# The last head pair's products with v of the first batch, moved ahead of late weight norms and of the second batch's scores in TensorE's order

## The chip, the cores and the metric

One core of a Trainium2 chip runs the whole program. Its engines each work through an instruction stream of their own, in order: TensorE (PE in the profile; its weight loads are listed as PEld), VectorE (DVE), ScalarE (ACT), GpSimd (POOL) and SyncE (SP, which here only starts DMA transfers). The metric is the device time of one execution in microseconds, taken as the median of several.

## The reference

Eight batches of sliding-window attention with position bias, whose output, laid out as 4608 tokens by 512 features, goes through a bilinear feed-forward layer:

```python
scores = scale * np.matmul(q, k.transpose(0, 1, 3, 2))          # 8 batches, 8 heads, 576 x 576, head size 64
scores = np.where(mask, scores + bias[None], -1000000000.0)     # window of 128 keys
attn = np.exp(scores - max); attn = attn / (sum + 1e-09)
x = np.matmul(attn, v)            # then (B*S, H*D) = (4608, 512)
out = (x @ w_a * (x @ w_b)) @ w_out    # 512 -> 1536 -> 512
```

All inputs are float32 numbers. The three weight matrices reach the kernel as the 64-bit integers that hold them.

## The kernel before

**Precision.** Each operand of the feed-forward layer is scaled by a power of two and split into a high and a low float16 part; three products (high·high, high·low, low·high) are added in PSUM. The scales come from norms: for each block of weights, squares are summed over the rows by a TensorE product with a matrix of ones (`up_norms`, line 152), VectorE takes the maximum (`up_scales`, line 158), GpSimd turns it into a power of two, and only then can the block be split.

**Preparing the weights.** There are 12 blocks f of the two up matrices and 6 pairs of blocks of the down matrix. For each block SP loads the raw words (line 119), ScalarE and VectorE take the words apart (lines 130, 131, 133), GpSimd adds two pieces (line 135, two instructions a block), ScalarE squares (line 141), TensorE sums the squares (line 156, four matmuls a block, called "norms" here), and after two blocks the four splits follow (ScalarE line 149, VectorE line 150). The norms of a pair of blocks, one even and one odd, share one PSUM tile `wn_ps`. The raw words lie in three buffers, so the load of block f+3 waits for the norms of block f. The whole is a Python generator, `weights`, of which other code draws steps.

**The first batch.** `first_attention` (line 526) runs batch 0 in float32 as 16 stages: 4 head pairs, 4 banks of query tiles each. A stage has the score products (line 569), bias and minimum on VectorE (line 580), exponentials on ScalarE (line 581), transposes of the probabilities on TensorE (line 587), and a copy of them out of PSUM (line 595). Behind the fourth bank of a pair come `pv`: reciprocals of the sums (lines 603, 604), a product that spreads them over PSUM (`rin_ps`, line 610), their copy to SBUF (ScalarE, line 614), the products with v (line 501, 14 float32 matmuls a pair; the trace has two records for each float32 matmul), and the scaled result x (VectorE, line 619), its squares (line 420 or 425) and, once all four pairs are there, the sum of squares over features (`n_ps`, line 515), the scale g of the hidden layer, and the split of x into `xs` (lines 435 and 436). The pairs' probabilities lie by turns in the buffers `phl` (pairs 0 and 2) and `pT` (1 and 3), so a product `x_ps<-pT,v` in the second half is that of the last pair. In each stage `other(0.5)` is called twice, which draws 0.75 steps of `weights` each.

**What sits in the same stretch.** Behind batch 0's attention come its up layer (`first_up`, line 836, products named `up_ps`), and woven into it the attention of batch 1 (`attention`, scores at lines 374 to 383) and the rest of `weights`.

**What sets the order.** The order in which the Python code emits is only a wish in this part: for TensorE, VectorE, ScalarE and GpSimd a scheduler places each instruction by its own estimate of when operands and buffers are ready, and by a priority (`tc.high_priority`). Only SP's order is kept as written here. From batch 1's feed-forward layer on TensorE's order is kept as written too. `tc.issue_after(i)` forbids the scheduler to place an instruction ahead of instruction i on its engine. PSUM has eight banks: two tagged `ch`, three `ef`, and three `at`. The `at` banks serve in turn the score tiles, the norms `wn_ps` and the two `n_ps` tiles of batch 0, which are opened when the first two pairs' squares are there and stay open until the last pair's are added.

Of the kernel before, what the change touches and what calls it, by code (L numbers as in the profile page):

```python
# [23 lines left out]
P = 128  # L24
NPAIR = H // 2
NKC = DM // P
# [16 lines left out]
PRIO = 2000  # L43
# [3 lines left out]
def attention_then_bilinear_ffn(ctx: ExitStack, tc: tile.TileContext, qT, kT, vP, w_a, w_b, w_out, rel, slopes2, outT):  # L47
# [104 lines left out]
    def up_norms(f, sq, ps):  # L152

        norms = ps[:, 2 * P * (f % 2):2 * P * (f % 2) + 2 * P].rearrange("p (m f) -> p m f", f=P)
        for c in range(NKC):
            pe.matmul(norms, ones16, sq[:, :, c * P:(c + 1) * P], start=(c == 0), stop=(c == NKC - 1))

    def up_scales(g, ps):

# [100 lines left out]

    class State:
        pass

    def load_v(b):

# [98 lines left out]
    def scores(o, bi):  # L364

        ps = ps_at.tile([P, 512], F32, tag="at", name="sc_ps")
        t = work.tile([P, 512], F32, tag="t", name="t", bufs=4)
        for i, c in BANKS[bi]:
            w = TILES[i][1]
            qq, kk = slice(64 * i, 64 * i + 64), slice(64 * i + 64 - w, 64 * i + 64)  # L370
            if o.b == 1:
                for e in range(2):
                    r = slice(64 * e, 64 * e + 64)
                    pe.matmul(ps[r, c:c + w], o.q[r, qq], o.k[r, kk], start=True, stop=True)
                continue
            for ks, last in ((o.kh, False), (o.kl, True)):
                for e in range(2):
                    pe.matmul(ps[64 * e:64 * e + 64, c:c + w], o.qs[:, e, qq], ks[:, e, kk], start=not last, stop=last)  # L378
        for i, c in BANKS[bi]:
            pc, w = TILES[i]  # L380
            n = o.n
            vec.tensor_tensor_reduce(out=t[:, c:c + w], in0=ps[:, c:c + w], in1=o.bias[:, WIN - w:WIN], scale=-0.125 if o.b == 1 else o.neg, scalar=3.0e38, op0=ALU.add, op1=ALU.min, accum_out=o.mn[:, n:n + 1])  # L382
            act.activation(t[:, c:c + w], t[:, c:c + w], AF.Exp, bias=o.mn[:, n:n + 1], scale=-1.0, accum_out=o.sm[:, n:n + 1])  # L383
            o.parts.append((n, t[:, c:c + w], pc, w))
            o.n += 1
# [104 lines left out]
    def each_pv(xp, vts, pts):  # L490

        for b in range(5):
            for rows, oc, blocks in by_keys(b):
                w = 64 * len(blocks)
                bank0, o0 = oc < 512, oc % 512
                first = oc == 0 if bank0 else b == 3
                last = b == 3 if bank0 else b == 4
                for n, (vt, pt) in enumerate(zip(vts, pts)):
                    for h in range(2):
                        c = 512 + 64 * h if b == 4 else 64 * (4 * h + b)  # L500
                        pe.matmul(xp[oc // 512][64 * h:64 * h + 64, o0:o0 + w], vt[0:rows, c:c + 64], probs(pt, rows, blocks, h), start=(n == 0 and first), stop=(n == len(vts) - 1 and last), skip_group_check=True)  # L501

    def pv(p, st, o, vhl):
        xp = new_x_ps()
# [19 lines left out]
    def first_attention(weights, rate):  # L524
# [74 lines left out]
        def pv(p, pt):  # L599


            rin = small.tile([P, QT], F32, tag="rin", name="rin0")
            vec.tensor_scalar(out=rin, in0=sums[p], scalar1=1e-9, scalar2=None, op0=ALU.add)
            vec.reciprocal(rin, rin)
            yield
            rp = [ps_ch.tile([P, 512], F32, tag="ch", name="rin_ps") for _ in range(2)]
            for i in range(QT):
                for e in range(2):
                    r = slice(64 * e, 64 * e + 64)
                    pe.matmul(rp[i // 8][r, 64 * (i % 8):64 * (i % 8) + 64], rin[r, i:i + 1].to_broadcast([64, 64]), ident[r, r], start=True, stop=True)  # L610
            r = first.tile([P, S], F32, tag="rin0", name="rin0", bufs=1)
            x = st.v[:, p, 0:S]
            for n, (c, w) in enumerate(halves_of_x):
                act.copy(r[:, c:c + w], rp[n][:, 0:w])
            xp = [ps_ch.tile([P, 512], F32, tag="ch", name="x_ps") for _ in range(2)]
            each_pv(xp, (st.v[:, p, :],), (pt,))
            yield
            for n, (c, w) in enumerate(halves_of_x):
                vec.scalar_tensor_tensor(out=x[:, c:c + w], in0=xp[n][:, 0:w], scalar=st.sv, in1=r[:, c:c + w], op0=ALU.mult, op1=ALU.mult)
            yield  # L620
            square_x(p, st, x, first if p == 2 else work if p == 3 else None)
            yield

        bias(0)
        n = 4 * NPAIR
        t = exponentials(0, 0, products(0, 0))
        beside = iter(())
        for k in range(n):
            p, bi = k // 4, k % 4
            ps = products((k + 1) // 4, (k + 1) % 4) if k + 1 < n else None  # L630
            other(0.5)
            if bi == 1 and p + 1 < NPAIR:
                bias(p + 1)
            tp = transposed(t)
# [7 lines left out]
                v_scale(st)  # L642
            if bi == 3:
                beside = pv(p, pts[p % 2])
            other(0.5)

        with tc.high_priority(offset=PRIO):
            next(beside)
        other(0.5)
        with tc.high_priority(offset=PRIO):  # L650
            for _ in beside:
                pass
            hidden_scale(st)
            for _ in split_x(st, True, False):
                pass
        states[0] = st

    def attention():
# [402 lines left out]
```

## Time and profile before

| | before |
|---|---|
| median of 3 runs | 1005.48 us (1005.28 to 1111.78) |
| the profiled execution: its own time | 1006.61 us |
| its span, first to last instruction | 1004.8 us |
| TensorE busy | 965.3 us, 96% |
| VectorE, ScalarE, GpSimd busy | 673.8, 649.2, 307.2 us |
| mean granted TensorE clock | 0.988 |

A row of the page or of a timeline gives start, duration, engine, source line, operation and tiles, and in brackets how long the engine had been idle before and what ended that. Rows of the window table give the busy time of each engine in a stretch of the span, and under PEclk the clock that TensorE was granted, 1.00 being full. Batch 0's attention takes the first 75 us or so, its feed-forward layer ends near 216 us, and the other seven batches fill the rest.

### The profile page before, as it was taken

The page shows a single profiled execution, that of the slowest core. Times are in us where ns is not written, and L with a number is a line of the kernel's source. Part 1 is how long each engine was busy: PE and PEld are TensorE (multiplying, and loading weights), DVE is VectorE, ACT ScalarE, POOL GpSimd, SP SyncE. Part 2 cuts the span into 40 slices and gives each one's busy share as a digit, 9 for nine tenths or more (in the row PEclk, how much of TensorE's full clock was granted, in tenths as well). Part 3 has the DMA queues.
Part 4 walks back from the last instruction along what each step waited for, and adds up shares of the span by engine and source line. Part 5 has one row for each costly group of instructions (what it writes and reads, how often), then busy time and mean ns, then how long its engine had stood idle before and what let it go on. Part 6 is the DMA issues. An engine that isn't in the chain of part 4 may idle for free.

```text
span 1004.8 us, 23888 instructions
## 1 busy us (share of the span) xinstructions
PE 965.3 (96%) x9339; PEld 750.9 (75%) x9339; DVE 673.8 (67%) x1833; ACT 649.2 (65%) x1715; POOL 307.2 (31%) x345
## 2 busy tenths in 40 slices
PE   7789879999999999999999999999999999999998
PEld 6567656777777777777787777777777777877776
DVE  5888999657878566775878687666677476524530
ACT  6886779657767756777767767677666766413321
POOL 3643463104565321352226112230223022211100
PEclk7799999999999999999999999999999999999999
DMA  8317733564444442472624642464326632210001
GB/s 318 119 74 266 234 112 73 124 166 81 100 90 96 141 90 43 97 172 66 126 49 107 172 90 45 95 178 107 80 62 106 161 67 43 49 37 7 2 13 36
DMA packets 148433, 102.83 MB, mean 102 GB/s; under 512 B 120032, under 2 KB 128352, under 8 KB 147296
## 3 DMA queue, kind: packets, MB, share of 16 engines
q1 hardware_dynamic: 138816, 91.77, 37.6%
q10 hardware_dynamic: 9504, 9.54, 2.9%
q8 instruction: 73, 1.20, 0.5%
q14 instruction: 40, 0.33, 0.1%
HBM read 48.33 MB, written 9.44 MB: 57 GB/s over the span
## 4 chain that ended last, share of the span: by engine, by line
PE 62%; DVE 11%; DMA 6%; ACT 6%; issue 2%; POOL 1%; SPq 0%; ACTq 0%; DVEq 0%
PE ch L836 19%; PE dn_ps L932 16%; PE p L836 14%; PE up_ps L836 8%; PE x_ps L501 3%; PE sc_ps L378 3%; DVE phl L400 2%; DMA pT<-phl 2%; DMA v<-in_vP 1%; DMA qk<-in_kT 1%; ACT phl L399 1%; DVE t L382 1%; ACT t L383 1%; DVE xs L436 1%; DMA qst<-qkl 1%
## 5 line engine op out<-in xcount | busy, mean ns | idle before, releaser
L836 PEld LDWEIGHTS <-wup 128*128 128x128 f16 x4224 | 407.9, 98 | 120.5 <-issue 14.8
L932 PE MATMUL dn_ps<-h,wdn 128*128 128x288 f16 x2016 | 254.3, 286 | 0.0
L932 PEld LDWEIGHTS <-wdn 128*128 128x128 f16 x2016 | 193.9, 98 | 51.8
L836 PE MATMUL ch<-xs,wup 128*128 128x288 f16 x1536 | 221.7, 286 | 0.9 <-ACT rc L861 0.6
L836 PE MATMUL up_ps<-xs,wup 128*128 128x288 f16 x1536 | 195.1, 286 | 6.1 <-DVE rc L785 4.6
L836 PE MATMUL p<-xs,wup 128*128 128x288 f16 x1152 | 172.6, 286 | 0.0
L891 POOL TENSOR_TENSOR rc<-rc,row 128x288 f32<-128x288 f32 x64 | 62.4, 975 | 279.7 <-DVE row L889 263.8
L400 DVE SCALAR_TENSOR_TENSOR phl<-t,rin,phl 128x192 f16<-128x192 f32 (+2 forms) x252 | 110.0, 477 | 18.9 <-ACT phl L399 18.7
L383 ACT ACTIVATE t<-t,mn 128x192 f32<-128x192 f32 (+2 forms) x252 | 107.2, 427 | 23.4 <-DVE mn L382 23.0
L829 ACT CAST h<-rc 128x576 f16<-128x576 f32 x96 | 64.2, 669 | 68.2 <-DVE rc L896 37.5
L399 ACT ACTIVATE phl<-t,rin 128x192 f16<-128x192 f32 (+2 forms) x252 | 88.7, 425 | 23.3 <-DMA pT<-phl 11.1
L830 DVE TENSOR_TENSOR h<-rc,h 128x576 f16<-128x576 f32 x90 | 71.2, 791 | 32.8 <-ACT h L829 32.0
L382 DVE CUSTOM_DVE_ANT_0 t<-sc_ps,bias,neg 128x192 f32<-128x192 f32 (+2 forms) x216 | 73.7, 389 | 8.4 <-PE sc_ps L378 8.4
L135 POOL TENSOR_TENSOR wup<-wup,wdn 128x512 int32<-128x512 int32 x36 | 54.7, 1541 | 45.6 <-ACT wdn L130 13.2
L937 ACT ACTIVATE row<-dn_ps,oi 128x288 f32<-128x288 f32 x56 | 27.7, 494 | 56.0 <-PE dn_ps L932 55.9
L873 ACT ACTIVATE row<-ch,g 128x288 f32<-128x288 f32 x64 | 31.9, 498 | 48.8 <-PE ch L836 48.8
L436 DVE TENSOR_TENSOR xs<-v,xs 128x576 f16<-128x576 f32 x52 | 48.4, 944 | 21.9 <-ACT xs L435 21.8
L360 POOL TENSOR_SCALAR bias<-rel_sb,ninv,sl_sb 128x192 f32<-128x192 f32 x24 | 21.4, 892 | 123.7 <-DVE mn L382 123.7
L868 DVE TENSOR_TENSOR rc<-p,rc 128x288 f32<-128x288 f32 x64 | 29.1, 454 | 44.1 <-PE p L836 34.8
L896 DVE SCALAR_TENSOR_TENSOR rc<-rc,g,ch 128x288 f32<-128x288 f32 x64 | 32.6, 510 | 23.6 <-PE ch L836 23.4
L383 ACT ACTIVATION_READ_ACCUMULATOR t<-t,mn 128x1 f32 x252 | 47.7, 189 | 0.0
L430 POOL TENSOR_TENSOR xq<-xq,sq 128x576 bf16<-128x576 bf16 x22 | 29.5, 1343 | 56.1 <-ACT sq L429 56.1
(151 smaller groups left out, 1311.7 us busy)
## 6 DMA issues: line engine op xcount, KB each, us to landing
v<-in_vP SPq DMA_DIRECT2D x8, 1280.0 KB, 6.0
out<-row ACTq DMA_DIRECT2D x60, 144.0 KB, 1.8
qk<-in_qT SPq DMA_DIRECT2D x28, 288.0 KB, 4.0
qk<-in_kT SPq DMA_DIRECT2D x28, 288.0 KB, 4.5
wdn<-in_w_a SPq DMA_DIRECT2D x12, 512.0 KB, 5.2
wdn<-in_w_b SPq DMA_DIRECT2D x12, 512.0 KB, 6.2
wdn<-in_w_out SPq DMA_DIRECT2D x12, 512.0 KB, 4.3
qst<-qkh SPq DMA_DIRECT2D x24, 144.0 KB, 2.8
```

The lines of the kernel that those rows point to most:

```text
L135: pool.tensor_tensor(out=t[:, m, :], in0=t[:, m, :], in1=low[:, m, :], op=ALU.add)
L382: vec.tensor_tensor_reduce(out=t[:, c:c + w], in0=ps[:, c:c + w], in1=o.bias[:, WIN - w:WIN], scale=-0.125 if o.b == 1 else o.neg, scalar= ...
L383: act.activation(t[:, c:c + w], t[:, c:c + w], AF.Exp, bias=o.mn[:, n:n + 1], scale=-1.0, accum_out=o.sm[:, n:n + 1])
L399: act.activation(phl[:, 0, pc:pc + w], e, AF.Copy, scale=s)
L400: vec.scalar_tensor_tensor(out=phl[:, 1, pc:pc + w], in0=e, scalar=s, in1=phl[:, 0, pc:pc + w], op0=ALU.mult, op1=ALU.subtract)
L436: vec.tensor_tensor(out=xs[:, n, 1, :, :], in0=src, in1=xs[:, n, 0, :, :], op=ALU.subtract)
L829: act.copy(h[:, f, :, 0, :], hid)
L830: eng.tensor_tensor(out=h[:, f, :, 1, :], in0=hid, in1=h[:, f, :, 0, :], op=ALU.subtract)
L836: pe.matmul(ps[:, 0:HT], wup[:, a[0], a[1], wi, k, :], xs[:, b, xi, k, :], start=(first and n == 0), stop=(last and n == len(ks) - 1), ski ...
L891: pool.tensor_tensor(out=x0, in0=x0, in1=mid, op=ALU.mult)
L896: vec.scalar_tensor_tensor(out=x1, in0=x1, scalar=st.g, in1=ch, op0=ALU.mult, op1=ALU.mult)
L932: pe.matmul(ps[:, 0:HT], wdn[:, f, wi, e * P:(e + 1) * P], h[:, f, t, hi, :], start=(m == 0 and n == 0), stop=(m == NF - 1 and n == 2))
```

## The change

`each_pv` returns its last matmul, and `first_attention` keeps that of the last head pair in `last_pv`. Two groups of instructions then may stand on TensorE only behind it: the norms of weight blocks whose step is drawn after that point, and all scores of batch 1. The draws themselves move too: stage 15, the last, no longer draws, and the draws around the last pair are put together into one, `other(1.0)`, behind the whole of the last pair's work with its hidden scale and split. The number of steps drawn in all stays 24.

```diff
     def up_norms(f, sq, ps):
...
-        for c in range(NKC):
-            pe.matmul(norms, ones16, sq[:, :, c * P:(c + 1) * P], start=(c == 0), stop=(c == NKC - 1))
+        with tc.issue_after(last_pv[0].ins) if last_pv[0] else ExitStack():
+            for c in range(NKC):
+                pe.matmul(norms, ones16, sq[:, :, c * P:(c + 1) * P], start=(c == 0), stop=(c == NKC - 1))
...
             if o.b == 1:
-                for e in range(2):
-                    r = slice(64 * e, 64 * e + 64)
-                    pe.matmul(ps[r, c:c + w], o.q[r, qq], o.k[r, kk], start=True, stop=True)
+                with tc.issue_after(last_pv[0].ins):
+                    for e in range(2):
+                        r = slice(64 * e, 64 * e + 64)
+                        pe.matmul(ps[r, c:c + w], o.q[r, qq], o.k[r, kk], start=True, stop=True)
...
-            each_pv(xp, (st.v[:, p, :],), (pt,))
+            last = each_pv(xp, (st.v[:, p, :],), (pt,))
+            if p == NPAIR - 1:
+                last_pv[0] = last
...
-            other(0.5)
+            if k < n - 1:
+                other(0.5)
...
-            other(0.5)
-
-        with tc.high_priority(offset=PRIO):
-            next(beside)
-        other(0.5)
+            if k < n - 1:
+                other(0.5)
+
         with tc.high_priority(offset=PRIO):
             for _ in beside:
                 pass
             hidden_scale(st)
             for _ in split_x(st, True, False):
                 pass
+        other(1.0)
```

Line numbers behind line 154 are larger by 1 to 7 in the changed kernel: norms 157, scores of batch 1 378, products with v 505, transposes 592, spread reciprocals 615, their copies 619, x 626, its squares 429 and 433.

The first place is TensorE's order after the last scores of batch 0, at the products with v of the third pair (`x_ps<-phl`). Before:

```order
L515 MATMUL n_ps<-xq,ones_73 128x512
L587 MATMUL tr_ps<-ident,t 128x128 x4
L515 LDWEIGHTS ones_73
L515 MATMUL n_ps<-xq,ones_73 128x64
L374 MATMUL sc_ps<-qkl,qkh 64x64 x2
L374 MATMUL sc_ps<-qkl,qkh 64x128 x2
L374 MATMUL sc_ps<-qkl,qkh 64x192 x2
L501 MATMUL x_ps<-phl,v 64x128 x4
L501 MATMUL x_ps<-phl,v 64x256 x4
```

The same place in the changed kernel:

```order
L520 MATMUL n_ps<-xq,ones_73 128x512
L592 MATMUL tr_ps<-ident,t 128x128 x4
L520 LDWEIGHTS ones_73
L520 MATMUL n_ps<-xq,ones_73 128x64
L505 MATMUL x_ps<-phl,v 64x128 x4
L505 MATMUL x_ps<-phl,v 64x256 x4
```

The first three score tiles of batch 1 (`sc_ps<-qkl,qkh`) have left this place; the norms of block 5, which stood just ahead of the first row before, have left it too.

The second place is TensorE's order at the last pair's products with v. Before, the norms of block 6 are the last thing ahead of them:

```order
L156 LDWEIGHTS ones_73
L156 MATMUL wn_ps<-wdn,ones_73 128x256
L501 MATMUL x_ps<-pT,v 64x128 x4
L501 MATMUL x_ps<-pT,v 64x256 x4
L501 MATMUL x_ps<-pT,v 64x128 x2
L501 MATMUL x_ps<-pT,v 64x64 x4
```

In the changed kernel products of the up layer stand ahead of them, and norms (of block 5) behind:

```order
L843 MATMUL up_ps<-xs,wup 128x288
L505 MATMUL x_ps<-pT,v 64x128 x4
L505 MATMUL x_ps<-pT,v 64x256 x4
L505 MATMUL x_ps<-pT,v 64x128 x2
L505 MATMUL x_ps<-pT,v 64x64 x4
L157 LDWEIGHTS ones_73
L157 MATMUL wn_ps<-wdn,ones_73 128x256
```

Ahead of the last pair's products stood, before, two groups of norms (blocks 5 and 6) and two of scores that now stand behind; the norms of blocks 6 and 7 and the scores follow among the next hundred matmuls of the up layer. Over the whole program both kernels issue the same instructions on every engine, and SP's order is the same.

The third place is ScalarE's order in the same stretch; `rin` with a number (745 before, 741 now) is the last pair's reciprocals, copied from PSUM. Before:

```order
L595 COPY pT<-tr_ps 128x512
L130 ACTIVATE wdn<-wdn 128x1024
L149 ACTIVATE wup<-wup,sup 128x2x256 x4
L383 ACTIVATE t,sm<-t,mn 128x64
L383 ACTIVATE t,sm<-t,mn 128x128
L383 ACTIVATE t,sm<-t,mn 128x192
L141 ACTIVATE wdn<-wup 128x2x512
L425 ACTIVATE sq<-v 128x576
L614 COPY rin_745<-rin_ps 128x512
L614 COPY rin_745<-rin_ps 128x64
L141 ACTIVATE wdn<-wup 128x2x512
```

In the changed kernel:

```order
L130 ACTIVATE wdn<-wdn 128x1024
L600 COPY pT<-tr_ps 128x512
L141 ACTIVATE wdn<-wup 128x2x512
L429 ACTIVATE sq<-v 128x576
L141 ACTIVATE wdn<-wup 128x2x512
L619 COPY rin_741<-rin_ps 128x512
L619 COPY rin_741<-rin_ps 128x64
```

The splits of line 149 and the exponentials of batch 1 have moved behind. The copy of transposed probabilities now stands behind a conversion of weights (line 130), and the two copies of the last pair's reciprocals stand behind the second squares of weights (line 141) instead of ahead of them.

More of the change, by code (lines that the diff above doesn't have):

```diff
@@ L262, in attention_then_bilinear_ffn @@
         pass
+    last_pv = [None]
     def load_v(b):
@@ L496, in each_pv @@
                 first = oc == 0 if bank0 else b == 3
-                last = b == 3 if bank0 else b == 4
+                ends = b == 3 if bank0 else b == 4
                 for n, (vt, pt) in enumerate(zip(vts, pts)):
@@ L500, in each_pv @@
                         c = 512 + 64 * h if b == 4 else 64 * (4 * h + b)
-                        pe.matmul(xp[oc // 512][64 * h:64 * h + 64, o0:o0 + w], vt[0:rows, c:c + 64], probs(pt, rows, blocks, h), start=(n == 0 and first), stop=(n == len(vts) - 1 and last), skip_group_check=True)
+                        last = pe.matmul(xp[oc // 512][64 * h:64 * h + 64, o0:o0 + w], vt[0:rows, c:c + 64], probs(pt, rows, blocks, h), start=(n == 0 and first), stop=(n == len(vts) - 1 and ends), skip_group_check=True)
+        return last
     def pv(p, st, o, vhl):
```

## The prediction

> **What bounds the kernel now.** I read the page first, then the windows, then TensorE's waits, then the timelines around the moved instructions.
>
> ```profile
> span 1004.8 us, 23888 instructions
> PE   7789879999999999999999999999999999999998
> 53.90:72.10 18.20, 13.82 (x157) 10.30 (x156) 14.79 (x34) 13.49 (x34) 9.31 (x12) 0.91 0.07 25
> 72.10:97.00 24.90, 24.90 (x212) 18.93 (x210) 22.11 (x46) 18.48 (x41) 7.15 (x8) 1.00 0.59 228
> 97.00:122.00 25.00, 21.74 (x178) 16.12 (x177) 23.97 (x44) 18.02 (x41) 10.56 (x10) 1.00 0.77 238
> 122.00:170.00 48.00, 39.47 (x392) 29.10 (x391) 45.81 (x101) 40.33 (x91) 25.69 (x19) 1.00 0.36 100
> 170.00:216.00 46.00, 44.06 (x451) 33.50 (x449) 28.54 (x98) 29.45 (x90) 8.52 (x7) 1.00 0.65 136
> ```
>
> After the stretch's length come busy TensorE, weight loads, VectorE, ScalarE and GpSimd, the granted clock and the transfers. TensorE is the bound nearly everywhere; a change that moves its instructions and adds none is worth what it takes from or adds to its idle time and its slow-clock time. There are two stages with such time near the change. From 53.9 to 72.1 TensorE is busy 13.82 of 18.2 us, at a mean clock of 0.91. From 97 to 170 it is idle 3.3 + 8.5 = 11.8 us, and there VectorE is busy 23.97 of 25 and 45.81 of 48: that stage belongs to VectorE, which prepares weights, evicts products and does batch 1's softmax. TensorE's waits in the two:
>
> ```profile
> PE up_ps L836 <- DVE rc L785: 4.6, 2, 2.3
> PE wn_ps L156 <- DVE mn L382: 3.1, 1, 3.1
> PE wn_ps L156 <- ACT wdn L141: 2.6, 3, 1.5
> PE wtot L101 <- ACT t L383: 1.8, 1, 1.8
> PE x_ps L501 <- DVE vhl L296: 1.5, 1, 1.5
> ```
>
> The second row is the one that the change touches: norms wait 3.1 us for the minima of batch 1's scores (line 382), which hold the one `at` bank that is left. Behind that wait stand the last pair's products:
>
> ```profile
> 53.87 0.61 PE L156 MATMUL wn_ps<-wdn,ones 128*128 128x256 bf16 x4
> 54.32 0.38 PE L515 MATMUL n_ps<-xq,ones 128*128 128x512 bf16 x1
> 56.07 0.88 PE L374 MATMUL sc_ps<-qkl,qkh 64*64 64x64 f32 x12 [0.40 <-DVE wtop L161]
> 56.87 1.97 PE L501 MATMUL x_ps<-phl,v 128*64 128x128 f32 x28
> 60.83 0.87 PE L374 MATMUL sc_ps<-qkl,qkh 64*64 64x192 f32 x8
> 61.53 1.25 PE L610 MATMUL rin_ps<-ident,rin 64*64 64x64 f32 x36
> 67.57 0.61 PE L156 MATMUL wn_ps<-wdn,ones 128*128 128x256 bf16 x4 [3.14 <-DVE mn L382]
> 68.11 3.34 PE L501 MATMUL x_ps<-pT,v 128*64 128x128 f32 x28
> 71.39 0.85 PE L156 MATMUL wn_ps<-wdn,ones 128*128 128x256 bf16 x4
> 72.08 1.63 PE L836 MATMUL up_ps<-xs,wup 128*128 128x288 f16 x12
> 66.00:68.00 2.00, 0.43 (x4) 0.31 (x4) 1.51 (x6) 1.57 (x4) 0.00 (x0) 1.00 0.00 0
> 70.00:72.00 2.00, 2.00 (x20) 1.55 (x17) 0.72 (x2) 0.46 (x2) 0.00 (x0) 0.52 0.00 0
> ```
>
> The same 28 records take 1.97 us for the third pair and 3.34 for the last: right after the 3.14 us of idle time the granted clock falls to 0.52. So the wait costs 3.14, and the slow clock 1.37 on these products, in all 4.5 us in front of the last x.
>
> **The change part by part.** *Removed.* The last pair's products no longer stand behind norms 5 and 6 and two groups of scores. Their own inputs are then late next: the copied reciprocals (ScalarE) and the transposed probabilities (VectorE, line 595). The rows that feed them:
>
> ```profile
> 55.33 0.68 DVE L161 TENSOR_REDUCE wtop<-wn_ps 128x4 f32<-128x512 f32 x1
> 55.93 1.21 DVE L133 SCALAR_TENSOR_TENSOR wup<-wdn,wup 128x1024 int32<-128x1024 int32 x1
> 57.06 1.40 DVE L150 SCALAR_TENSOR_TENSOR wup<-wup,sup 128x512 f16<-128x512 f32 x2
> 59.72 0.68 DVE L131 TENSOR_SCALAR wup<-wdn 128x1024 int32<-128x1024 int32 x1
> 63.16 3.80 DVE L150 SCALAR_TENSOR_TENSOR wup<-wup,sup 128x512 f16<-128x512 f32 x3
> 71.28 0.94 DVE L619 SCALAR_TENSOR_TENSOR v<-x_ps,sv,rin 128x512 f32<-128x512 f32 x2 [2.60 <-PE x_ps L501]
> 62.77 2.98 POOL L135 TENSOR_TENSOR wup<-wup,wdn 128x512 int32<-128x512 int32 x2 [0.17 <-issue]
> 56.17 0.57 ACT L595 COPY pT<-tr_ps 128x512 f32<-128x512 f32 x1
> 56.63 1.20 ACT L130 ACTIVATE wdn<-wdn 128x1024 int32<-128x1024 uint32 x1
> 63.70 0.67 ACT L614 COPY rin<-rin_ps 128x512 f32<-128x512 f32 x2
> 65.78 1.06 ACT L141 ACTIVATE wdn<-wup 128x1024 bf16<-128x1024 f32 x1 [1.42 <-POOL wup L135]
> ```
>
> *Added.* On ScalarE the copies (0.67) stood ahead of the second line-141 squares; now they stand behind them, and those wait for GpSimd's second pair of adds, which waits for VectorE's second line 133. So the chain is: VectorE starts its first line 133 at 55.4 (the maximum of line 161 at 55.33 no longer stands ahead of it) and ends it at 56.6; two splits 1.40, line 131 0.68, a small sum 0.2 and the second line 133 1.21 bring it to 60.1. GpSimd's first pair of adds runs beside this; the row at 63.16 has three splits beside such a pair in 3.80, 1.27 each, against 0.7 each at 57.06, so three instructions beside adds cost up to 1.6 more: 60.1 to 61.7. Adds 2.98: 63.1 to 64.7. Squares 1.06: 64.2 to 65.8. Copies 0.67: 64.8 to 66.4. TensorE could start the last pair there; it waited for its norms until 68.11 before. I take 66.2, toward the upper end, since the row at 63.16 has the same two engines on the same kinds of instructions. At 1.97 us the products end at 68.2, against 71.45 (68.11 + 3.34): the last x comes 3.2 us earlier (2.9 to 4.7 by the ends).
>
> For the new gaps: at the third pair TensorE now waits for the copy of line 595, behind line 130 on ScalarE: 56.17 + 1.20 + 0.57 = 57.9, where it started at 56.87; the scores that filled this place are gone, so 2.2 us are idle from 55.7. The third pair then ends at 59.9, transposes and 12 up products take the 2.0 that lie between 58.84 and 60.83 before, and the spread reciprocals wait for VectorE until 61.3 to 62.9 (second line 133, then x of the third pair): up to 1.0 idle; with their 1.25 and six up products (0.8) the last pair's place is reached at 64 to 65: up to 1.4 idle. None is as long as 3.14, the one length that the trace shows with a fall of the clock; its bound is therefore 0 to 1.37 us for one group of products, and I take 0, with the upper end in the range. [...]
>
> *Moved, TensorE.* From 53.87 TensorE has, in the changed order, the last pair done at 68.2, then norms 5, and goes on with the 12 products of the up layer when x is scaled: 68.2 + 0.94 = 69.1. At this place it stood at 72.08 before. But it owes what has moved behind: scores 0.80 (56.07 to 56.87) and 0.70 (60.83 to 61.53), norms 6 0.54 (67.57 to 68.11) and norms 7 at full clock 0.45 (53.87 to 54.32), 2.5 in all. 69.1 + 2.5 = 71.6 against 72.08: a gain of 0.5, by the ends of the chain from 1.9 gained to 1.1 lost (66.4 + 1.97 + 1.37 + 0.94 + 2.5 = 73.2).
>
> *Moved, VectorE.* It too has done less at its line 619:
>
> ```profile
> L150 DVE SCALAR_TENSOR_TENSOR wup<-wup,sup x20: 734/744/1780, 52.9 to 132.0; 128x512 f16<-128x512 f32 x20
> L382 DVE CUSTOM_DVE_ANT_0 t<-sc_ps,bias 128x192 f32<-128x192 f32 x22 | 7.2, 347 | 0.0
> 76.23 0.33 SPq L268 DMA_DIRECT2D v<-in_vP  x1
> 147.85 2.27 POOL L830 TENSOR_TENSOR h<-rc,h 128x576 f16<-128x576 f32 x1
> ```
>
> It owes one maximum 0.68, three splits at 0.74, five minima at 0.35 at most: 4.7 us. It gets 3.2 of it back by starting line 619 earlier, and is 1.5 us behind. From 72.1 to 97 it had 24.9 - 22.11 = 2.8 us of idle time, which can take this debt, as far as the work is there to be done; what is left meets the stage from 97 to 170 where it is full. Bounds: 0 to 1.5 us lost; I take 0.5.
>
> *Queues passed.* SP's order is the same, but its transfer of v for batch 1 at 76.23 waits for the last split of x (line 436), and the raw words of blocks 8 to 10 are queued behind it. With x 3.2 us earlier it starts near 73. That gives nothing by itself where VectorE is full; it is a rival below. Behind it the load of block 10 waits for norms 7, now about 83 on TensorE instead of 72; the transfers before it still run until then. GpSimd's order moves one line 830 (2.27) from between its last adds of weights, at 147.85, to a later place: 0 to 2.3 us gained ahead of the scale of the down weights (`wtot`, 1.8 us of TensorE waiting). I count nothing, because VectorE feeds those adds.
>
> *Sum.* -0.5 + 0.5 = 0 us. From 216 us on nothing is changed, so the rest passes through as it is. The profiled execution has 1006.61 us (1004.8 of span), the median of the runs is 1005.48; taking the change from either gives the same time, and I forecast against the median: **1005.5 us**. A difference of less than 2%, about 20 us, is what a measurement of this kernel would call no change.
>
> **The rivals.** *Forecast, no change (chance 0.50):* 1004 to 1007. The 4.5 us in front of the last x go, but some 4 us of new, shorter waits come, on ScalarE and VectorE.
>
> *Faster, the early x feeds the weights (0.25).* The transfer of v and of the raw words starts 3.2 us earlier, the weights of blocks 8 to 10 are ready earlier, and TensorE's 11.8 us of waits from 97 to 170 shrink by that: 1005.5 - 3.2 = 1002, at best 1005.5 - 4.5 = 1001. For it speaks that norms wait 2.6 us for squares of weights; against it that VectorE, which takes the words apart, has no free time there (45.81 of 48).
>
> *Slower, ScalarE's order gives the gain back and VectorE's debt arrives whole (0.22).* Place: the copies behind line 141. If the last pair's products start no earlier than 68.11, the point from which it decides, TensorE owes 2.5 us with only the 1.37 of the slow clock saved, and VectorE's 4.7 us come into its full stage with at most 2.8 taken by idle time: 1005.5 + 1.2 to 1005.5 + 4.7, the middle about 1008.5. For it speaks the chain above, whose upper end lies only 1.7 us below 68.11. [...]
>
> *The change does not reach the chip as written (0.03):* the order shows that it does; what is left here are effects far from the place, at either sign.
>
> **How the numbers follow.** The likeliest case gives 1005.5. The range takes the faster case to 1001.5 and the slower to 1009.0; it leaves out about 0.1. Nothing in these cases comes near 20 us, so within 2% has 0.97, faster 0.01, slower 0.02, the last for disturbed runs such as the 1111.78.
>
> **What the profile will show.** If I am right, the wait of `wn_ps` for line 382 near 64 us is gone; the last pair's products start at 65 to 67 and take about 2.0 us; just ahead of them ScalarE's line 141 waits for GpSimd; the third pair's products start near 57.9 after an idle 2 us; and TensorE's waits from 97 to 170 sum to 11 to 13 us. A last pair at 68 or later, or a clock of 0.5 there, means the slower case; waits of under 9 us from 97 to 170 mean the faster one. The forecast is wrong if the span moves by more than 4 us, or if idle time changes behind 216 us.

## The result, and the profile after

The changed kernel is slower: 1013.92 us (median of 6 runs, 1011.36 to 1015.38) against 1004.96 us for the kernel before beside it. The ratio is 1.0089 (95% interval 1.0074 to 1.0104), about 9 us. That is within 2%, as predicted, but above the predicted range (1001.5 to 1009.0), and no case with a sizeable chance held it. One execution of the kernel before (1111.78 us) and one of the first experiment (1643.23 us) ran in a slow state of the chip and are left out of the ratios. The profiled execution of the changed kernel has 1014.11 us of its own; the first line of its page and its windows, in the columns of the prediction:

```profile
span 1012.3 us, 23889 instructions
53.90:72.10 18.20, 13.74 (x139) 10.28 (x139) 12.02 (x20) 8.92 (x17) 7.67 (x10) 0.81 0.06 24
72.10:97.00 24.90, 24.81 (x211) 18.47 (x209) 22.15 (x51) 20.41 (x52) 9.74 (x10) 1.00 0.65 235
97.00:122.00 25.00, 21.85 (x172) 15.39 (x170) 24.48 (x46) 18.61 (x42) 10.97 (x9) 0.93 0.66 206
122.00:170.00 48.00, 38.23 (x378) 28.22 (x377) 44.03 (x103) 39.32 (x89) 24.87 (x19) 1.00 0.40 112
170.00:216.00 46.00, 42.76 (x414) 32.06 (x412) 25.53 (x83) 27.42 (x80) 8.03 (x7) 0.96 0.45 95
```

TensorE's clock is lower in the first stretch (0.81 against 0.91), in the third (0.93 against 1.00) and, which the prediction never looked at, in the last (0.96 against 1.00), where TensorE also does less (42.76 against 44.06 us). TensorE's timeline around the change:

```profile
55.53 1.97 PE L505 MATMUL x_ps<-phl,v 128*64 128x128 f32 x28
62.98 2.18 PE L615 MATMUL rin_ps<-ident,rin 64*64 64x64 f32 x36 [3.42 <-DVE v L626]
65.57 1.63 PE L843 MATMUL up_ps<-xs,wup 128*128 128x288 f16 x6
67.12 2.58 PE L505 MATMUL x_ps<-pT,v 128*64 128x128 f32 x28
```

The wait of 3.14 us for the minima of batch 1's scores is gone, and a wait of 3.42 us ahead of the spread reciprocals has come; the products behind it run slowly again (2.18, 1.63 and 2.58 us, at full clock 1.25, 0.9 and 1.97). So little was lost or won here. To see where the 9 us come from I compare the two traces: the start of a group of TensorE in after, less that of the same group in before. From the second row on TensorE has done the same work ahead of the group in both; at the first, after still owes the scores and norms that were moved, 2.5 us by the prediction's count. The last of these groups is batch 1's up layer, here after and then before:

```profile
224.50 1.63 PE L843 MATMUL up_ps<-xs,wup 128*128 128x288 f16 x12 [0.28 <-DVE row L827]
```

```profile
215.69 1.63 PE L836 MATMUL up_ps<-xs,wup 128*128 128x288 f16 x12 [0.28 <-DVE row L820]
```

| place on TensorE | before | after is later by |
|---|---|---|
| last pair's products with v | 68.11 | -1.0 |
| batch 1's scores, second pair | 95.98 | 1.4 |
| batch 1's scores, third pair | 129.28 | 2.7 |
| first product with the down weights | 169.88 | 4.4 |
| batch 2's first scores | 188.19 | 4.8 |
| batch 1's up layer | 215.69 | 8.8 |

Behind 216 us it no longer grows (the spans differ by 7.5 us). Half of it arises between 170 and 216 us. Of the edited lines only batch 1's last scores run there, more than 100 us behind the matmul that they may not pass. TensorE's and ScalarE's timelines there, after:

```profile
168.76 3.10 PE L843 MATMUL up_ps<-xs,wup 128*128 128x288 f16 x24 [2.67 <-ACT rc L790]
205.30 2.77 PE L505 MATMUL x_ps<-pT,vhl 128*64 128x128 f16 x42 [3.08 <-DMA pT<-phl]
208.00 3.27 PE L819 MATMUL dn_ps<-h,wdn 128*128 128x288 f16 x24
158.45 5.62 ACT L231 ACTIVATE wdn<-wup,ratio 128x512 f16<-128x512 f32 x9
165.64 2.35 ACT L403 ACTIVATE phl<-t,rin 128x64 f16<-128x64 f32 x7
168.33 0.67 ACT L790 COPY rc<-up_ps 128x288 f32<-128x288 f32 x2
191.21 1.16 ACT L324 ACTIVATE qkl<-qk 128x1152 bf16<-128x1152 f32 x1 [4.33 <-DMA qk<-in_kT]
193.79 1.49 ACT L403 ACTIVATE phl<-t,rin 128x192 f16<-128x192 f32 x4 [0.45 <-DVE rin L400]
195.80 5.11 SPq L409 DMA_TRANSPOSE pT<-phl  x1
```

and before:

```profile
167.48 1.63 PE L836 MATMUL up_ps<-xs,wup 128*128 128x288 f16 x12 [0.60 <-ACT rc L783]
197.05 1.51 PE L501 MATMUL x_ps<-pT,vhl 128*64 128x128 f16 x42
155.15 2.37 ACT L399 ACTIVATE phl<-t,rin 128x64 f16<-128x64 f32 x7 [0.19 <-DVE rin L396]
160.31 6.83 ACT L230 ACTIVATE wdn<-wup,ratio 128x512 f16<-128x512 f32 x11
183.93 1.49 ACT L399 ACTIVATE phl<-t,rin 128x192 f16<-128x192 f32 x4 [0.45 <-DVE rin L396]
185.94 5.41 SPq L405 DMA_TRANSPOSE pT<-phl  x1
189.03 1.16 ACT L321 ACTIVATE qkl<-qk 128x1152 bf16<-128x1152 f32 x1 [3.61 <-DMA qk<-in_kT]
```

Two places on ScalarE differ. **The squares**: the squares of batch 2's second pair of q and k (line 324, 321 before) wait for a transfer. Before, they stood behind the last normalisations of batch 1 (line 403, 399 before); after, they stand ahead of them, and ScalarE holds the normalisations back. So the last transpose of batch 1's probabilities starts at 195.80 instead of 185.94, TensorE waits 3.08 us for it, and its next products run at a slower clock (0.50 from 204.95 to 208.36 us; 2.77 against 1.51 us). **The copy**: in both kernels a copy of up products out of PSUM (line 790, 783 before) stands behind eleven splits of down weights (line 231, 230 before). The seven normalisations, which stood ahead of the splits before, now stand between the splits and the copy, and TensorE waits 2.67 us for it instead of 0.60. No line of either place is in the diff. The scheduler, which places each instruction by its own estimate of readiness, put them in another order although the edit applies some 100 us further up: on ScalarE and VectorE the two orders differ up to about 195 us, on TensorE up to 186, behind that nowhere.

### The profile page after: what moved, and what is told of

The parts are those of the page before. It is cut to its first block, busy times and chain, and to the rows that moved or that the text cites. A ratio compares the mean times of both kernels' runs of the same rounds, so it can differ in the third digit from the quotient of the medians.

```text
span 1012.3 us, 23889 instructions
## 1 busy us (share of the span) xinstructions
PE 971.5 (96%) x9339; PEld 753.6 (74%) x9339; DVE 673.1 (66%) x1833; ACT 649.0 (64%) x1715; POOL 306.8 (30%) x345
## 4 chain that ended last, share of the span: by engine, by line
PE 71%; DVE 11%; ACT 8%; DMA 6%; issue 2%; POOL 1%; SPq 0%; ACTq 0%; DVEq 0%; POOLq 0%
PE ch L843 18%; PE dn_ps L939 17%; PE p L843 13%; PE up_ps L843 11%; PE x_ps L505 4%; PE sc_ps L382 3%; DVE phl L404 2%; DMA pT<-phl 2%; PE dn_ps L819 2%; ACT phl L403 1%; DMA v<-in_vP 1%; DVE xs L440 1%; POOL wup L135 1%; DMA qk<-in_kT 1%; DVE wup L150 1%
## 5 line engine op out<-in xcount | busy, mean ns | idle before, releaser
L843 PE MATMUL up_ps<-xs,wup 128*128 128x288 f16 x1536 | 198.0, 288 | 7.1 <-DVE rc L792 3.7
L505 PE MATMUL x_ps<-pT,vhl 128*64 128x128 f16 (+2 forms) x1176 | 44.2, 232 | 5.3 <-DMA pT<-phl 3.1
L505 PEld LDWEIGHTS <-vhl 128*64 128x64 f16 x1176 | 41.5, 113 | 9.8 <-issue 3.3
```

The source lines that it names most:

```text
L505: last = pe.matmul(xp[oc // 512][64 * h:64 * h + 64, o0:o0 + w], vt[0:rows, c:c + 64], probs(pt, rows, blocks, h), start=(n == 0 and first ...
L843: pe.matmul(ps[:, 0:HT], wup[:, a[0], a[1], wi, k, :], xs[:, b, xi, k, :], start=(first and n == 0), stop=(last and n == len(ks) - 1), ski ...
```

## The experiments

The theory after the result: most of the loss is in these two places, far from the change (*far*). The rivals: it is in the wait and the slow clock near the last pair (*local*), or in VectorE's work, which the change delays in its full stage (busy 45.81 of 48 us in before; *VectorE*). All ratios below are to the kernel before on the same chip, with the 95% interval; executions of one kernel scatter by 1 to 6 us, so the lateness of a single profile and the median can differ by some us. Lateness is that of the table above, against the same profile of before. Each run's rows have the line numbers of its own kernel, a few lines from those of after.

**The squares put back.** One row moves on ScalarE, and one on VectorE:

```diff
-        act.activation(lo.bitcast(BF16), qk, AF.Square, accum_out=sums)
+        with tc.issue_after(last_norm[1, 3].ins) if (b, p) == (2, 1) else ExitStack():
+            act.activation(lo.bitcast(BF16), qk, AF.Square, accum_out=sums)
...
-            act.activation(phl[:, 0, pc:pc + w], e, AF.Copy, scale=s)
+            last_norm[o.b, o.p] = act.activation(phl[:, 0, pc:pc + w], e, AF.Copy, scale=s)
```

> After, with one instruction moved: on ScalarE the squares of batch 2's second q/k pair (line 324 of after) may only stand behind batch 1's last normalisation (line 403). Far theory: in after these squares stand ahead and wait 4.33 us for a transfer, so the last transpose of probabilities starts at 195.80 and TensorE waits 3.08 us at 205.30 and then runs 1.26 us longer at a slow clock. With the squares behind, the transpose starts near 190, the wait is gone, and 4.3 us come back: 1013.9 - 4.3 = 1009.6 (1008.5 to 1010.7). Local theory: what was lost was lost near 60 us, and the wait at 205 only stands where another one would be: no change, 1013 to 1015.

Measured: 1009.88 us, 1.0040 (1.0025 to 1.0056). The last products with v of batch 1 no longer wait:

```profile
200.46 1.51 PE L509 MATMUL x_ps<-pT,vhl 128*64 128x128 f16 x42
```

Some 5 of the 9 us are this one instruction, with the VectorE row that follows it. The other 4 are there by 188 us (3.4 late).

**The squares put ahead in the kernel before.** The counterpart: the squares are emitted one step earlier, and batch 1's last normalisations may not stand ahead of them. Nothing near the last pair changes.

```diff
             load(i + 2)
+            if i == 3:
+                ready = squares(5)
...
-                nxt = squares(i + 1)
+                nxt = squares(i + 1) if i != 4 else ready
...
+            with tc.issue_after(early[0].ins) if early else ExitStack():
+                act.activation(phl[:, 0, pc:pc + w], e, AF.Copy, scale=s)
```

> Before, with the same one instruction moved the other way: on ScalarE the squares of batch 2's second q/k pair stand ahead of batch 1's last normalisation. Far theory: they start at 189.0 when their transfer has landed, the normalisation follows at 190.3 instead of 183.9, the transpose starts near 192.4 instead of 185.94 and lands 7.4 us later, at 199.8, where TensorE stands ready at 197.05: a wait of 2.7 us and up to 1.3 us of slow clock, 1005.0 + 2.7 to 4.0 = 1007.7 to 1009.0. Local theory: within 1 us of before, 1004 to 1006.

Measured: 1011.21 us, 1.0059 (1.0046 to 1.0072), more than expected. The same wait appears, though all but this row and a VectorE row behind it have the order of the kernel before, and TensorE runs more slowly just behind it (24 products with the down weights take 4.32 us, 3.11 in before):

```profile
189.29 1.16 ACT L323 ACTIVATE qkl<-qk 128x1152 bf16<-128x1152 f32 x1 [6.05 <-DMA qk<-in_kT]
202.17 1.92 PE L506 MATMUL x_ps<-pT,vhl 128*64 128x128 f16 x42 [3.30 <-DMA pT<-phl]
204.02 4.32 PE L820 MATMUL dn_ps<-h,wdn 128*128 128x288 f16 x24
```

At 188 us it is 0.7 late, at 216 us 6.3. Removing and adding the cause both show 5 to 6 us: this part is settled.

**The two halves of the order, crossed.** Seven of the kernels from here on hold the engines' orders to written lists of instruction numbers. The lists set only the order of issue and add no waits:

```diff
+    held = {EngineType.DVE: [...], EngineType.Activation: [...], EngineType.PE: [...]}
+    for numbers in held.values():
+        for a, z in zip(numbers, numbers[1:]):
+            tc.add_manual_dep(placed[f"I-{z}"], f"I-{a}", DependencyInfo(NoSync, DATA), reason="held")
```

The first has after's order up to 72 us and before's behind it; the second is the reverse.

> The instructions of TensorE, VectorE, ScalarE and GpSimd are held in a given order: that of after up to the split of the last pair's x (about 72 us), that of before for all that is left. Far theory: most of the loss goes, since the local part is worth only about +1 at 72 us and at most some us of VectorE's owed work: 1005 to 1008. Local theory (the 3.42 us wait, the slow clock and the owed work cost the 9 us): 1011 to 1015.

Measured: 1012.13 us, 1.0068 (1.0056 to 1.0080): a miss for the far theory. Its loss is all there at 96 us (5.2 late), and nothing comes behind it. Between 72 and 97 us TensorE is now idle for 2.6 us, at a lower clock:

```profile
72.10:97.00 24.90, 22.27 (x164) 15.88 (x165) 19.11 (x49) 18.54 (x51) 4.24 (x6) 0.86 0.57 223
72.01 0.87 PE L377 MATMUL sc_ps<-qkl,qkh 64*64 64x192 f32 x8 [0.92 <-DVE mn L385]
74.46 0.82 PE L157 MATMUL wn_ps<-wdn,ones 128*128 128x256 bf16 x3 [1.59 <-DVE mn L385]
```

Neither kernel has these waits. At the seam the scores and norms that after had postponed follow one another closely, and these wait for the minima ahead of them. So the seam makes a loss of its own, and this run tells nothing about local against far.

> The reverse: the order of before up to the last pair's x (about 72 us), that of after for all that is left. Far theory: most of the loss stays although nothing is changed around the last pair: 1010 to 1014. Local theory: 1004 to 1006.

Measured: 1016.22 us, 1.0107 (1.0091 to 1.0124), more than expected. With before's order around the last pair and after's behind it, the whole loss appears (5.6 late at 188 us, 10.5 at 216). So it does not need the local wait of 3.42 us. This seam too can add a loss of its own (2.0 late at 96 us, where after is 1.4 late), so the run does not say how the 9 us divide.

The third holds after's order up to 158 us, where the two orders have much the same work left, and before's behind it:

> The order of after is held up to about 158 us on all four engines, that of before for what is left (so the eleven splits of the down weights, line 231, stand behind the seven normalisations and a copy of up products as they do in before, and the squares of batch 2's second q/k pair behind the last normalisation). Far theory: the waits of 2.67 us at 168.76 and of 3.08 us with its slow clock at 205.30 both go, what stays is the 2.3 to 2.7 us by which TensorE is late at 131 us: 1007 to 1008.5. Local theory: 1011 to 1015. If an order taken over from another timing brings waits of its own, as in the run that changes over at 72 us, 1009 to 1011.

Measured over 12 runs: 1006.68 us (1003.69 to 1009.96), 1.0010 (0.9998 to 1.0022), slightly less than the far theory expected. So about 8 of the 9 us are in the order behind 158 us. The profile is of one of the slower executions (1008.47 us, 4.1 late at 216 us). The wait for the copy is not gone, since before's order also has a copy behind eleven splits, and after's earlier half reaches it late:

```profile
170.58 1.84 PE L842 MATMUL up_ps<-xs,wup 128*128 128x288 f16 x7 [2.94 <-ACT rc L789]
```

**The local wait taken away.** The squares as in the first run, and VectorE's and ScalarE's orders near the last pair held so that the third pair's x, the reciprocals and the copy of transposed probabilities stand ahead of the weights' lines 131 and 133, and the last pair's copied reciprocals ahead of the second line 141; some of GpSimd's memsets move ahead of its second adds with this:

> The first experiment (squares behind the last normalisation) with the local wait taken away too: on VectorE the third pair's x, the reciprocals of the last pair and the copy of its transposes are held ahead of lines 131 and 133 of the weights, and on ScalarE the copies of the spread reciprocals ahead of the second squares of weights. The last pair's products should start near 62.5 instead of 66 to 67, without the 3.42 us wait and with a full clock. Local theory: that gains 3 to 4.5 us against the first experiment: 1005.5 to 1007. Theory that VectorE's full stage (97 to 170) takes every local gain: within 1 us of the first experiment, 1009 to 1011, and TensorE, early at 72 us, is as late at 131 us as before.

Measured: 1007.25 us, 1.0019 (1.0010 to 1.0027), between the two expectations. The last pair starts 3.4 us earlier than in after, at full clock (1.00 from 53.90 to 72.10 us):

```profile
61.44 1.26 PE L618 MATMUL rin_ps<-ident,rin 64*64 64x64 f32 x36 [2.42 <-DVE v L629]
63.72 1.97 PE L508 MATMUL x_ps<-pT,v 128*64 128x128 f32 x28
```

Against the two runs with the squares alone put back (1.0040, and 1.0034 below) this is worth 1.5 to 2 us. At 216 us the kernel is still 2.9 late.

> The local repair, the order of after up to 158 us, the order of before behind it. If the three causes (local wait, copy behind the down weights' splits, squares ahead) add up, this is 1004 to 1006, the level of before; if VectorE's full stage takes the local gain it equals the run that changes over at 158 us without the repair, 1007 to 1008.5.

With the local repair, after's order up to 158 us and before's behind it: 1004.62 us, 0.9994 (0.9985 to 1.0004). The lateness at 216 us is -0.6. All of the loss is gone. The last pair starts 5.4 us earlier than before, with 2.5 us of moved work still owed; at 96 us, at equal work, TensorE is 3.1 us ahead, and at 170 us 0.6. So the stage between, where VectorE has little idle time (busy 24.26 of 25 us from 97 to 122, 42.35 of 48 from 122 to 170), takes most of the lead back.

**The copy.** The squares as in the first run; in addition ScalarE's order around 160 us is held so that the normalisations and both copies stand ahead of or between the eleven splits, and VectorE's rows follow in the same way. Beside it on the same chip, the first run's kernel again:

> The first experiment (squares behind), and around 160 us the seven normalisations of the third pair and two copies of up products (line 790) no longer stand behind the eleven splits of the down weights on ScalarE (line 231) but ahead of and between them; VectorE's row follows in the same way; TensorE's order is that of after. In the run that took over before's order at 158 us the wait for this copy was still there, 2.94 us, since before too has a copy behind eleven splits. If the wait at 168.76 is what is left of the loss there, it goes (at most 0.5 us is left of 2.67) and the time falls by 2 to 2.7 us against the first experiment in the same call: a ratio of 1.001 to 1.002 to before. If TensorE then only waits longer for VectorE or for the down weights at the first product of the down layer: no change, 1.003 to 1.005.

> The first experiment once more, beside the run with the copies between the splits: a ratio of 1.0025 to 1.0055 to before, as the first time.

Measured: 1006.96 us, 1.0014 (1.0005 to 1.0023), against 1008.61 us, 1.0034 (1.0022 to 1.0046). The two, in this order:

```profile
163.44 3.11 PE L842 MATMUL up_ps<-xs,wup 128*128 128x288 f16 x24
180.48 1.54 PE L504 MATMUL x_ps<-pT,vhl 128*64 128x128 f16 x42 [1.46 <-DMA pT<-phl]
```

```profile
166.20 3.10 PE L847 MATMUL up_ps<-xs,wup 128*128 128x288 f16 x24 [2.66 <-ACT rc L794]
```

The wait goes, 2.76 us are gained there (163.44 against 166.20), and 1.46 given back as a wait at later products with v. The difference of the medians is 1.65 us; the intervals just touch, so this share is the least certain.

**One half of the change.** The scores' constraint alone, with norms and draws as before, leaves the norms where the scheduler wants them:

```diff
-        with tc.issue_after(last_pv[0].ins) if last_pv[0] else ExitStack():
-            for c in range(NKC):
-                pe.matmul(norms, ones16, sq[:, :, c * P:(c + 1) * P], start=(c == 0), stop=(c == NKC - 1))
+        for c in range(NKC):
+            pe.matmul(norms, ones16, sq[:, :, c * P:(c + 1) * P], start=(c == 0), stop=(c == NKC - 1))
...
```

The other half needs no run. With the norms' constraint alone every engine's order is that of after, with the moved draws alone that of before: the norms' constraint is the whole change.

> Of the change only the scores of batch 1 are held behind the last pair's products; the norms and the draws stay as in before. In the order that comes out the down weights' splits and the squares of batch 2's second q/k pair stand ahead of the normalisations, as in after. Far theory: at least the 4 to 6 us of these two places are lost, 1009 to 1014, although no wait of 3.4 us for the third pair's x need be there. Local theory: 1003 to 1007.

Measured: 1009.09 us, 1.0035 (1.0022 to 1.0048). The last pair starts 5.2 us earlier than before, and at 188 us TensorE is still 1.6 ahead. But the squares have jumped ahead here too, and at 216 us it is 3.9 behind:

```profile
62.90 1.97 PE L504 MATMUL x_ps<-pT,v 128*64 128x128 f32 x28
199.24 1.62 PE L504 MATMUL x_ps<-pT,vhl 128*64 128x128 f16 x42 [3.24 <-DMA pT<-phl]
200.79 4.64 PE L818 MATMUL dn_ps<-h,wdn 128*128 128x288 f16 x24
```

> The scores part of the change alone, and the squares of batch 2's second q/k pair held behind batch 1's last normalisation on ScalarE. In the run of the scores part alone TensorE was 1.6 us earlier than before at batch 2's first scores and 3.9 us later at batch 1's feed-forward layer, with a wait of 3.24 us for the last transpose in between. Far theory: that wait goes and the lead of 1.6 us stays: 1003.5 to 1004.5. If another wait stands behind it (the third transpose was late too, 0.77 us): 1005 to 1006.

This half with the squares put back: **1003.39 us over 12 runs (1002.32 to 1006.03), 0.9986 (0.9977 to 0.9995)**. It is faster than the kernel before, by 1.4 us. The last pair starts 5.3 us earlier; at 96 us, at equal work, TensorE is 3.3 us ahead, and 1.5 of it arrive at 216 us. The wait for the last transpose is gone:

```profile
196.16 1.51 PE L508 MATMUL x_ps<-pT,vhl 128*64 128x128 f16 x42
```

> The scores part alone, its order held up to about 158 us, the order of before behind it, so that the down weights' splits and the squares both stand behind the normalisations. In the run of the scores part alone TensorE was 2.3 us earlier than before at 157.6 us. Far theory: this lead is kept to the end, 1002.5 to 1003.5, faster than before. If the copy of up products (line 790 of after) or VectorE holds TensorE back near 168, as in the local repair with this order, no more than 0.6 us is left: 1004.5 to 1005.5.

The same half up to 158 us and before's order behind it: 1004.19 us, 0.9985 (0.9976 to 0.9993). The expected 1002.5 to 1003.5 was not reached; the lead of 2.5 us at 129 us is 1.3 at 170.

**The account.** Of 0.0089, the squares take about 0.0052 (1.0089 to 1.0040 and 1.0034, the mean 1.0037); the rest of the order between 158 and 195 us, of which the copy is the visible part, 0.0020 to 0.0027 (the copy run, and the runs with before's order from 158 us); the local wait 0.0015 to 0.0021. The sum, 0.009 to 0.010, is the whole; each share is the difference of two ratios with intervals of 0.001 to 0.0015 to either side.

## Why the prediction was wrong

**The step that failed** is the sum, -0.5 + 0.5 = 0 us, together with the step that closes it: "From 216 us on nothing is changed, so the rest passes through as it is." That sentence itself held: behind 195 us no engine's order differs. But the sum stopped at 72 us for TensorE and counted, for the 140 us between, only VectorE's debt and one row of GpSimd's; it put the new order of that stretch at nothing without a reason. In that stretch the changed kernel's ScalarE and VectorE have another order, and the order from 158 to 195 us alone costs 7 to 8 of the 9 us, 5 of them in one instruction. "Queues passed" should have listed, for every engine and to the end of the difference, each instruction that waits for a transfer and now stands ahead of work it stood behind. Line 324 is such a row, with its price in the trace of before: line 321 waits 3.61 us for `qk<-in_kT` and runs at 189.03, 5.1 us behind the normalisations that after puts behind it. The case that came true is the one of 0.03, "effects far from the place".

**The third pair** started at 55.53, not 57.9: it did not wait for the copy of line 595. That copy fills `pT`, the other buffer; the third pair reads `phl`. The premise was wrong. The idle time that I had spread over three gaps (2.2, 1.0 and 1.4, in all 4.6) came as 0.8 and 3.42, in all 4.2: the sum was right, the place was not, and **in one piece it slowed the clock** in after's execution (0.50 for 6.83 us from 61.59).

**The clock**: I counted 0, with 1.37 as the bound. In after's execution four groups lost 0.92 + 0.24 + 0.73 + 0.61 = 2.5 us; in the runs that share this local order it was 0 to 2.5. The bound was that of one group, though the slow clock went on over what followed, in after for 6.83 us.

**The last pair**: 66.2 predicted, 67.12 in after with its slow clock, 65.81 and 66.00 in the two runs of after with the squares put back. The copies of the reciprocals (64.8 to 66.4) came just behind the upper end of the chain. While GpSimd's adds ran, the two splits took 2.45 us, and line 131 behind them 2.05; in before they took 1.40 and 0.68, line 131 there beside adds as well (58.48 to 61.55). That is 2.4 more, where the prediction allowed 1.6. GpSimd's second adds were faster (2.53 for 2.98):

```profile
64.89 1.06 ACT L141 ACTIVATE wdn<-wup 128x1024 bf16<-128x1024 f32 x1 [1.06 <-POOL wup L135]
65.85 0.68 ACT L619 COPY rin<-rin_ps 128x512 f32<-128x512 f32 x2
```

**TensorE's -0.5** held as a number: at 96 us the four runs with after's local order and its order behind it (the two with the squares put back, the copy run, and the one held to 158 us) stand at -0.2, -0.6, -0.4 and -0.5. After itself stands at 1.4; it lost 2.5 us to the slow clock near the last pair, the four 0 to 1.6.

**VectorE's debt**, taken as 0.5 of 0 to 1.5: from 96 to 129 us after loses 1.3, the run held to 158 us 2.5, the copy run 1.4, the two with the squares put back 2.3 and 1.6. So 1 to 2 us more than the term were lost in its stretch, but that VectorE's debt is the reason is not shown. In these five traces, at equal work, TensorE's idle time in the stretch changes by -0.4 to 0.8 us and its busy time grows by 1.4 to 1.7, because of one slow piece (in after 0.50 for 3.41 us from 105.96; in the two with the squares put back and the copy run 36 up products near 125 us take 6.12 to 6.24 us, 4.58 at full speed, and in the run held to 158 us 27 take 5.14, 3.47 at full speed). The same 48 up products in before, in after, and in the run with the squares put ahead, which has before's order here:

```profile
104.31 6.05 PE L836 MATMUL up_ps<-xs,wup 128*128 128x288 f16 x48
```

```profile
106.80 7.29 PE L843 MATMUL up_ps<-xs,wup 128*128 128x288 f16 x48
```

```profile
104.06 7.72 PE L844 MATMUL up_ps<-xs,wup 128*128 128x288 f16 x48
```

This last run loses nothing by 129 us (-0.3 late at both ends): its idle time is shorter by as much. Whether the clock or VectorE costs the 1 to 2 us in the others stays open.

**The rivals.** The waits from 97 to 170 us are 3.15 + 9.77 = 12.9 us, within the 11 to 13 of the forecast: the faster case did not come, although v's transfer did start at 73.18 as said. The slower case named the copies behind line 141 as its place and a last pair at 68.11 or later as its condition. The copies did stand behind line 141, but the last pair started at 67.12, so the condition did not come, and the case is no better confirmed than the forecast, though its sign was right. Two of the prediction's ends are slightly off in its own terms: 2.5 less 1.37 is 1.1, not 1.2, and the last x comes at least 3.1 us earlier, not 2.9. Neither changes the range.

## What to carry to other kernels

Where a scheduler places instructions by its own estimates, a constraint at one place can re-order in-order engines far behind it. Compare the order of every engine down to the last difference, and look first for an instruction that waits for a transfer and now stands ahead of work on the way to the bound; pin those few, and then measure the edit itself. A start 5 us earlier, 3 of them at equal work, was worth 1.4 us here: the next stage, where another engine was nearly full (VectorE, busy 45.81 of 48 us in before), took back most of it.

## What the runs showed of the hardware that was not expected

**The same idle time can cost the clock or not.** With 3.42 us idle ahead of the spread reciprocals, after loses 2.5 us at once. The first run, with 3.42 us too, loses 1.4 a little later (six up products 1.63, the last pair 2.63), and the same kernel, run again, loses 1.6 from the spread reciprocals on (1.90). In the run held to 158 us what follows is at full speed (clock 1.00 from 53.90 to 122.00 us):

```profile
62.56 1.26 PE L614 MATMUL rin_ps<-ident,rin 64*64 64x64 f32 x36 [3.42 <-DVE v L625]
```

Between 50 and 990 us the granted clock is 1.00 in the traces of before and after, but for four pieces at 0.50: 3.41 us from 68.51 in before, and in after 6.83 us from 61.59, 3.41 us from 105.96 and 3.41 us from 204.95. The three of after start whole multiples of 3.41 us apart (13 and 29 times). In the 3.41 us just ahead of each of the four TensorE was busy for 0.68 to 1.55 us; in steps of 3.41 us from these starts, no other stretch of the two traces has it busy for less than 1.68 us. In before the 3.14 us lie mostly in one such stretch. In the run held to 158 us the 3.42 us are shared by two, with TensorE busy for 1.57 and 1.83 us; the steps of this run are placed by its slow products from 146.33 us on, 25 steps behind 60.97 (three up products take 0.90 us there, 0.53 at full speed). That the place of the idle time in these steps decides is a reading of these three traces; no run isolates it. Before, and then the run held to 158 us (TensorE's busy time stands behind the length, the clock third from the end):

```profile
65.08:68.49 3.41, 0.92 (x11) 0.69 (x12) 2.60 (x7) 2.04 (x5) 0.67 (x1) 1.00 0.00 0
68.49:71.90 3.41, 3.41 (x29) 2.44 (x26) 0.81 (x2) 1.68 (x5) 0.00 (x0) 0.50 0.00 0
```

```profile
57.56:60.97 3.41, 1.57 (x14) 1.08 (x11) 3.38 (x4) 1.06 (x1) 2.41 (x4) 1.00 0.00 0
60.97:64.39 3.42, 1.83 (x42) 1.57 (x43) 2.32 (x5) 0.68 (x1) 2.49 (x3) 1.00 0.01 2
```

Shorter waits came ahead of a slow piece too. In after, waits of 0.53 and 1.45 us share the stretch from 102.55 to 105.96 us (1.55 us busy), and the clock behind it is 0.50; ahead of 204.95, where it is 0.50 next, lies most of the wait of 3.08 us. One slow piece takes up to 1.7 us of TensorE's time (an estimate: half of 3.41), and the mean granted clock of one kernel's executions varies: 0.983 to 0.993 in the twelve of the run held to 158 us, of which the one at 0.983 is the slowest (1009.96 us).

**A small VectorE instruction lasted until a whole row of GpSimd's had ended.** In the run with the local repair, the addition ahead of the reciprocals (9 columns), 0.15 us in after, took 2.29 us, to 60.52. It ended with GpSimd's last memset, at 60.50. The rows of that run, and then that of after:

```profile
58.23 2.29 DVE L611 TENSOR_SCALAR rin<-sm 128x9 f32<-128x9 f32 x1
56.07 3.38 POOL L135 TENSOR_TENSOR wup<-wup,wdn 128x512 int32<-128x512 int32 x2 [5.63 <-DVE wup L133]
59.40 1.10 POOL L998 MEMSET phl<- 128x128 f16 x5
```

```profile
60.85 0.15 DVE L608 TENSOR_SCALAR rin<-sm 128x9 f32<-128x9 f32 x1
```

The repair with before's order behind 158 us shows it again: 1.64 us, to 59.56, where the memsets end at 59.53. The ends suggest that GpSimd's row held the addition, which no run isolates; if it did, it held it here over an add and several memsets in a row. In before the same addition took 0.78 us, beside adds that ran on to 61.55. So an instruction of 0.15 us in after stood for 2.29 us in the chain ahead of the last pair.
